# Attention decode with gated GLU on one core: V loads on GpSimd's software queue, K loads and weights on SyncE, w_down in 14 tiles of 128 rows

## The chip, the cores and the metric

The kernel runs on one core of a Trainium2 chip. The metric is the device time of one execution, in microseconds (us). Times are quoted as medians. On one core an execution counts as slow when it is over 1.5% above the fastest of the same kernel. A ratio is the mean time of one kernel's fast runs over that of the other's fast runs in the same rounds on the same chip, so it is not quite the ratio of the medians that stand beside it. Spans in the profile are about 2 us shorter than the device time.

## The reference

Two layers over the same weights and caches; x is [4, 1, 512].

```python
x = A_x
for layer in range(2):            # written out twice in the reference
    n = layernorm(x)
    q = (n @ wq) -> 32 heads of 128                    # 4 heads share one of 8 K/V heads
    p = softmax(q . k_cache * 128**-0.5)               # 4 batches x 8 heads x 4096 keys x 128
    x = x + (p . v_cache) @ wo
    n = layernorm(x)
    x = x + (sigmoid(n @ w_gate) * (n @ w_up)) @ w_down   # 512 -> 1792 -> 512
```

The caches are 33.5 MB each, in bf16, and do not fit on the core, so both layers read them whole: 134 of the 148 MB that the kernel moves. The weights (14 MB) are loaded once and stay.

## The kernel before

The work goes in 16 groups: 2 layers of 8 K/V heads. A group needs four K tiles and four V tiles of 1 MB, one for each batch. All 128 tiles pass through a ring of 10 buffers in the order of use: K of group 0, V of group 0, K of group 1, and so on. A tile takes the buffer of the tile ten places before it and waits until that one has been used. The four K buffers of a group come free when its scores are done, the four V buffers when its values are done.

```python
NS = 10
wd = sb("wd", [FR, 4, 4, D], bf)                 # FR = 112 partitions
...
def load_kv(n, kind, b):
    s = len(tiles) % NS                           # the buffer, in turn
    tiles.append((n, kind, b))
    ...
    if kind == "k":                               # 128 rows of 8 KB
        i = A_k[b, g].rearrange("(p t) d -> p (t d)", p=P)
        o = dst[:]
    else:                                         # 512 rows of 2 KB
        i = A_v[b, g].rearrange("(a p t) d -> p a (t d)", a=4, p=P)
        o = dst[:].rearrange("p (a x) -> p a x", a=4)
    S.put("sp", lambda e: e.dma_start(o, i), writes=[f"r{s}"], dma=f"r{s}")
...                                               # weights: also S.put("sp", ...)
for n, (l, g) in enumerate(groups):
    ensure_t(n, range(B))       # VectorE transposes K blocks in place
    scores(n)                   # TensorE; frees four K buffers
    pump()                      # issue the loads whose buffer is now used: K,K of n+1, V,V of n+1
    softmax(n)
    ...
    values(n)                   # TensorE; frees four V buffers
    pump()                      # V,V of n+1, then K,K of n+2
    merge(n); y_proj(n)
    if last: ... glu(...)       # end of a layer: projection, layer norm, GLU, layer norm
```

Of the kernel before, what the change touches and what calls it, by code (L numbers as in the profile page):

```python
# [10 lines left out]
ENGINES = ("sp", "act", "pe", "dve", "pool")  # L11
# [80 lines left out]
def bass_interleave_layers__gqa_block_cached__glu_gated_glu__decode_kernel(nc, A_x, A_k, A_v, A_wq, A_wo, B_x, B_wg, B_wu, B_wd, out):  # L92
    B, SQ, D = A_x.shape
# [4 lines left out]
    P = 128  # L98
# [3 lines left out]
    NLAYER = 2  # L102
    NQ = 4
    FS = F // 4
    FR = FS // 4
    scale = float(DH) ** -0.5
    eps = 1e-5
    NS = 10

    S = _Sched()  # L110
# [3 lines left out]
    def sb(name, shape, dtype=dt.float32):  # L114
        return es.enter_context(nc.sbuf_tensor(name, list(shape), dtype))

    def ps(name, shape, dtype=dt.float32):
        return es.enter_context(nc.psum_tensor(name, list(shape), dtype))

    bf = dt.bfloat16  # L120
    ring = [sb(f"ring{i}", [P, T * DH], bf) for i in range(NS)]
    wq = sb("wq", [P, KD, H * DH], bf)
    wo = sb("wo", [P, H, D], bf)
    wg = sb("wg", [P, KD, F], bf)
    wu = sb("wu", [P, KD, F], bf)
    wd = sb("wd", [FR, 4, 4, D], bf)

    x_io = sb("x_io", [P, D], bf)
    x_row = [sb(f"x_row{i}", [P, D]) for i in range(2)]
# [12 lines left out]
    oT = sb("oT", [P, H, B], bf)  # L142
    t_sb = sb("t_sb", [P, FS])
    h_sb = sb("h_sb", [P, FS], bf)
    hT = sb("hT", [P, 4, 4, B], bf)

    ml = sb("ml", [P, 64])
    tr = sb("tr", [P, 64])
# [12 lines left out]
    sel_h = sb("sel_h", [P, 16], bf)  # L161
# [6 lines left out]
    M_ps = ps("M_ps", [P, 512])  # L168
    Y_ps = ps("Y_ps", [P, 512])

    sem_names = list(ENGINES) + [f"r{i}" for i in range(NS)] + [f"wq{i}" for i in range(4)]
    sem_names += [f"wo{i}" for i in range(4)] + ["wg", "wu", "wd", "xin", "out"]
    sems = {k: es.enter_context(nc.semaphore(f"sem_{k}")) for k in sem_names}


# [34 lines left out]
    def load_kv(n, kind, b):  # L210
        s = len(tiles) % NS
        tiles.append((n, kind, b))
        slots[n, kind, b] = s
        dst = ring[s]
        g = groups[n][1]
        if kind == "k":
            i = A_k[b, g].rearrange("(p t) d -> p (t d)", p=P)
            o = dst[:]
        else:
            i = A_v[b, g].rearrange("(a p t) d -> p a (t d)", a=4, p=P)  # L220
            o = dst[:].rearrange("p (a x) -> p a x", a=4)
        S.put("sp", lambda e: e.dma_start(o, i), writes=[f"r{s}"], dma=f"r{s}")  # L222

    def pump():
        while queue:
            if isinstance(queue[0], tuple):
                m = len(tiles) - NS
                if m >= 0 and tiles[m] not in used:
                    return
                load_kv(*queue.pop(0))  # L230
            else:
                queue.pop(0)()

    def load_w(key, o, i):
        S.put("sp", lambda e: e.dma_start(o, i), writes=[key], dma=key)  # L235

    wq_src = A_wq.rearrange("(p k) n -> p k n", k=KD)

    def load_wq(i):
        load_w(f"wq{i}", wq[:, :, i * 1024:(i + 1) * 1024], wq_src[:, :, i * 1024:(i + 1) * 1024])  # L240

    def load_wo(i):
        load_w(
            f"wo{i}", wo[:, i * 8:(i + 1) * 8, :],
            A_wo[i * 8 * P:(i + 1) * 8 * P, :].rearrange("(h p) n -> p h n", p=P),
        )
# [7 lines left out]
        (3, "v"): [lambda: load_wo(2)],  # L254
        (4, "v"): [lambda: load_wo(3)],
        (5, "v"): [lambda: load_w("wg", wg[:], B_wg.rearrange("(p k) n -> p k n", k=KD))],
        (6, "v"): [lambda: load_w("wu", wu[:], B_wu.rearrange("(p k) n -> p k n", k=KD))],
        (7, "k"): [lambda: load_w(
            "wd", wd[:].rearrange("r j c n -> r j (c n)"), B_wd.rearrange("(j r c) n -> r j (c n)", j=4, c=4)
        )],  # L260
    }
    queue.append(lambda: load_wq(0))
    for n in range(len(groups)):
# [10 lines left out]
    def layer_norm():  # L274
        xi = state["x"]
        xr = x_row[xi][0:B, :]
        S.put("dve", lambda e: e.bn_stats(stats[0:B, :], xr), reads=[f"x{xi}"], writes=["stats"])
        S.put("dve", lambda e: e.bn_aggr(mv[0:B, :], stats[0:B, :]), reads=["stats"], writes=["mv"])
        S.put("dve", lambda e: e.tensor_scalar_add(vpe[0:B, :], mv[0:B, 1:2], eps), reads=["mv"], writes=["vpe"])
        S.put(  # L280
            "pool", lambda e: e.tensor_tensor(rstd[0:B, :], vpe[0:B, :], mhalf[0:B, :], ALU.pow),
            reads=["vpe", "mhalf"], writes=["rstd"],
        )
        S.put(
            "dve",
            lambda e: e.tensor_scalar(  # L286
                xn[0:B, :], xr, mv[0:B, 0:1], rstd[0:B, :], op0=ALU.subtract, op1=ALU.mult
            ),
            reads=[f"x{xi}", "mv", "rstd"], writes=["xn"],
        )  # L290
        fns = []
        for k in range(KD):
            fns.append(lambda e, k=k: e.matmul(  # L293
                M_ps[:, k * B:(k + 1) * B], lhsT=xn[0:B, bass.ds(k, P, step=KD)], rhs=sel_h[0:B, 0:B],
                start=True, stop=True,
            ))
        S.put("pe", fns, reads=["xn", "sel_h"], writes=["M"])
        S.put(
            "dve", lambda e: e.tensor_copy(xnT[:].rearrange("p k b -> p (k b)"), M_ps[:, 0:KD * B]),
            reads=["M"], writes=["xnT"],  # L300
        )
# [150 lines left out]
    def residual(mult):  # L452
        xi = state["x"]
        S.put(
            "dve",
            lambda e: e.scalar_tensor_tensor(  # L456
                out=x_row[1 - xi][0:B, :], in0=Y_ps[0:B, :], scalar=mult, in1=x_row[xi][0:B, :],
                op0=ALU.mult, op1=ALU.add,
            ),
            reads=["Y", f"x{xi}"], writes=[f"x{1 - xi}"],  # L460
        )
        state["x"] = 1 - xi

    def glu(hooks):
        layer_norm()
        hooks[0]()
        for w, key, bank, bkey in ((wg, "wg", PT_ps, "PT"), (wu, "wu", O_ps, "O")):
            fns = []
            for k in range(KD):
                for j in range(4):  # L470
                    fns.append(lambda e, k=k, j=j, w=w, bank=bank: e.matmul(  # L471
                        bank[32 * j:32 * j + B, 0:FS], lhsT=xnT[:, k, :], rhs=w[:, k, j * FS:(j + 1) * FS],
                        start=(k == 0), stop=(k == KD - 1),
                    ))
            S.put("pe", fns, reads=["xnT", key], writes=[bkey])
        S.put("act", lambda e: e.activation(t_sb[:], PT_ps[:, 0:FS], ACTF.Tanh, scale=0.5), reads=["PT"], writes=["t"])
        S.put(
            "dve",
            lambda e: e.scalar_tensor_tensor(
                out=h_sb[:], in0=t_sb[:], scalar=1.0, in1=O_ps[:, 0:FS], op0=ALU.add, op1=ALU.mult  # L480
            ),
            reads=["t", "O"], writes=["h"],
        )
        fns = []
        for c4 in range(4):
            fns.append(lambda e, c4=c4: e.matmul(
                M_ps[0:FR, c4 * 16:(c4 + 1) * 16], lhsT=h_sb[:, bass.ds(c4, FR, step=4)], rhs=sel_h[:],
                start=True, stop=True,
            ))
        S.put("pe", fns, reads=["h", "sel_h"], writes=["M"])  # L490
        S.put(
            "dve", lambda e: e.tensor_copy(hT[0:FR].rearrange("p c j b -> p (c j b)"), M_ps[0:FR, 0:64]),
            reads=["M"], writes=["hT"],
        )
        hooks[1]()
        fns = []
        for j in range(4):
            for c4 in range(4):
                fns.append(lambda e, j=j, c4=c4: e.matmul(  # L499
                    Y_ps[0:B, :], lhsT=hT[0:FR, c4, j, :], rhs=wd[:, j, c4, :],  # L500
                    start=(j == 0 and c4 == 0), stop=(j == 3 and c4 == 3),
                ))
        S.put("pe", fns, reads=["hT", "wd"], writes=["Y"])
        residual(0.5)


# [10 lines left out]
    for n, (l, g) in enumerate(groups):  # L517
        last = g == G - 1
        ensure_t(n, range(B))
        scores(n)  # L520
        used.update((n, "k", b) for b in range(B))
        pump()
        softmax(n)
        if not last:
            q_proj(g + 1)
        probs_t(n)
        weights(n)
        values(n)
        used.update((n, "v", b) for b in range(B))
        pump()  # L530
        merge(n)
        y_proj(n)
        if last:
            ensure_t(n + 1, [0, 1])
            residual(1.0)
            glu([lambda: ensure_t(n + 1, [2]), lambda: ensure_t(n + 1, [3])])
            if l + 1 < NLAYER:
                layer_norm()
                q_proj(0)
# [4 lines left out]
          writes=["out"], dma="out")  # L544
# [41 lines left out]
```

## Time and profile before

415.18 us, median of two runs (414.91 to 415.44). The execution that was profiled is a third one, 417.68 us.

| what | before | view |
|---|---|---|
| bytes moved | 148.4 MB | page, queues |
| DMA share 90% or more | in 35 of 40 slices | page, slices |
| K to landing, V to landing | 14.2 us, 16.2 us | page, DMA issues |
| w_down to landing | 30.9 us | page, DMA issues |
| rate while w_down passes | 221 to 280 GB/s | table of stretches |
| hole at the layer boundary | 238 to 248 us, 21 GB/s | table of stretches |

These are the lines of the page for slices of 10.4 us, counted from 0 (the first line in tenths of busy time, the second in GB/s) and for DMA issues (target, source, issuer, count, size, median us from issue to landing):

```profile
DMA  7999999999999999999999919999999999999500
GB/s 260 408 382 413 386 389 406 391 415 386 406 391 394 403 407 415 396 416 281 293 411 396 359 25 392 407 401 405 401 407 399 407 399 407 400 407 399 209 2 0
...
ring<-in_A_k_cache_dram SPq DMA_DIRECT2D x64, 1024.0 KB, 14.2
ring<-in_A_v_cache_dram SPq DMA_DIRECT2D x64, 1024.0 KB, 16.2
```

The kernel is bound by its transfers. The engines are at 90% or more in nearly every slice. The rate dips in slices 18 and 19 although the engines are full, and it falls to 25 GB/s in slice 23. The last slices are the chain of work after the last transfer.

The table of stretches gives, for each stretch, busy time of PE, PEld (TensorE's products and its weight loads), DVE, ACT and POOL (VectorE, ScalarE, GpSimd), TensorE's granted clock (as a share of full speed), DMA share and GB/s:

```profile
190.00:195.00 5.00, 0.00 (x0) 0.00 (x0) 3.49 (x2) 0.00 (x0) 0.00 (x0) 0.50 1.03 230
195.00:200.00 5.00, 0.00 (x0) 0.00 (x0) 2.00 (x2) 0.00 (x0) 0.00 (x0) 0.50 1.02 221
200.00:205.00 5.00, 3.59 (x32) 0.94 (x32) 1.30 (x2) 0.00 (x0) 0.00 (x0) 0.50 1.04 280
...
238.00:248.00 10.00, 5.25 (x74) 2.34 (x72) 2.99 (x7) 1.04 (x5) 0.54 (x1) 0.66 0.05 21
```

The two dips differ. In the first three lines the DMA share is 1.02 to 1.04 at 221 to 280 GB/s: the engines work, but badly. That is w_down on 112 partitions. In the last line the share is 0.05: the engines have nothing to do. The ten buffers are full, and the next one comes free only with the first scores of layer two, which stand behind the GLU.

### The profile page before, as it was taken

Reading aid. Unit: us, or ns where it says so; the run is one execution under the profiler, and the core shown is the slowest. Engines: PE = TensorE matmul, PEld = TensorE weight load, DVE = VectorE, ACT = ScalarE, POOL = GpSimd, SP = SyncE. Lnnn points to the kernel's source line nnn. Section 1 sums busy time; section 2 is a strip of 40 time slices with the busy share of each in tenths; the row PEclk is TensorE's granted clock in tenths of the full one; section 3 lists DMA queues with packets and bytes.
Section 4 is the critical chain, followed back from the end, with each engine's and each line's share of the span. In section 5 each row is a group of like instructions: output and inputs, shape, how many; then the busy total and the mean of one; then the engine's idle time right before and its main releaser. Section 6 shows DMA issues by size and latency. Waiting matters only on the chain.

```text
span 415.9 us, 4348 instructions
## 1 busy us (share of the span) xinstructions
PE 203.4 (49%) x1784; PEld 84.8 (20%) x1784; DVE 205.9 (50%) x259; ACT 82.5 (20%) x179; POOL 6.7 (2%) x24
## 2 busy tenths in 40 slices
PE   0047343473545447352316745475745555654556
PEld 0013111121212212120002222131312222221122
DVE  3823627346272825516316626473829283838221
ACT  1031040210403031040210014132231303030300
POOL 4000000000000000000000000000000000000000
PEclk9985565555555555555555766655556666566659
DMA  7999999999999999999999919999999999999500
GB/s 260 408 382 413 386 389 406 391 415 386 406 391 394 403 407 415 396 416 281 293 411 396 359 25 392 407 401 405 401 407 399 407 399 407 400 407 399 209 2 0
DMA packets 50067, 148.40 MB, mean 357 GB/s; under 512 B 2232, under 2 KB 6336, under 8 KB 41600
## 3 DMA queue, kind: packets, MB, share of 16 engines
q1 hardware_dynamic: 50048, 148.13, 93.6%
q8 instruction: 14, 0.23, 0.2%
q14 instruction: 5, 0.04, 0.0%
HBM read 148.12 MB, written 0.00 MB: 356 GB/s over the span
## 4 chain that ended last, share of the span: by engine, by line
issue 40%; DMA 28%; PE 14%; DVE 7%; SPq 6%; ACT 4%; POOL 0%; POOLq 0%; ACTq 0%; DVEq 0%
DMA ring<-in_A_k_cache_dram 24%; PE S_ps L342 5%; SPq L222 5%; DMA ring<-in_A_v_cache_dram 5%; DVE ring L333 3%; PE O_ps L413 3%; ACT p_sb L358 2%; PE Y_ps L499 2%; PE M_ps L429 1%; DVE ml L352 1%; SPq L235 1%; PE Y_ps L446 1%; PE PT_ps L471 1%; PE O_ps L471 1%; ACT o_sb L424 1%
## 5 line engine op out<-in xcount | busy, mean ns | idle before, releaser
L333 DVE STREAM_TRANSPOSE ring<-ring 128x2048 int32<-128x2048 int32 x64 | 146.2, 2299 | 53.7 <-DMA ring<-in_A_k_cache_dram 53.3
L342 PE MATMUL S_ps<-ring,qbd 128*16 128x512 bf16 x512 | 57.0, 620 | 82.4 <-DVE ring L333 81.4
L358 ACT ACTIVATE p_sb<-S_ps,nbias 128x1024 bf16<-128x1024 f32 x16 | 40.4, 2522 | 185.8 <-DVE nbias L355 185.8
L413 PE MATMUL O_ps<-ring,pt_sb 128*16 128x512 bf16 x512 | 57.3, 628 | 27.4 <-ACT pt_sb L374 15.9
L352 DVE TENSOR_REDUCE ml<-S_ps 128x1 f32<-128x1024 f32 x16 | 19.6, 1224 | 60.9 <-PE S_ps L342 60.9
L342 PEld LDWEIGHTS S_ps<-ring,qbd 128*16 128x16 bf16 x512 | 15.4, 120 | 121.2 <-DVE ring L333 81.5
L429 PE MATMUL M_ps<-sel_o,o_sb 128*128 128x16 f32 x128 | 26.9, 349 | 14.0 <-ACT o_sb L424 14.0
L429 PEld LDWEIGHTS M_ps<-sel_o,o_sb 128*128 128x128 f32 x128 | 25.3, 294 | 28.5 <-ACT o_sb L424 28.5
L317 PE MATMUL Q_ps<-qT,perm 128*128 128x16 bf16 x64 | 4.4, 179 | 51.5 <-ACT qT L314 51.5
L446 PE MATMUL Y_ps<-wo,oT 128*4 128x512 bf16 x64 | 26.5, 560 | 4.7 <-ACT oT L435 4.7
L413 PEld LDWEIGHTS O_ps<-ring,pt_sb 128*16 128x16 bf16 x512 | 15.8, 125 | 56.9 <-issue 38.8
L379 DVE STREAM_TRANSPOSE tr<-ml 128x64 f32<-128x64 f32 x16 | 3.9, 245 | 42.2 <-ACT qT L314 37.0
L424 ACT ACTIVATE o_sb<-O_ps,wcol 128x512 f32<-128x512 f32 x16 | 11.0, 687 | 68.3 <-PE O_ps L413 64.6
L323 ACT ACTIVATE qbd<-Q_ps 32x64 bf16<-32x64 f32 x64 | 13.7, 214 | 6.6 <-PE Q_ps L317 6.0
L317 PEld LDWEIGHTS Q_ps<-qT,perm 128*128 128x128 bf16 x64 | 2.9, 107 | 52.8 <-ACT qT L314 52.8
L369 PE MATMUL PT_ps<-sel_p,p_sb 128*128 128x64 bf16 x128 | 9.4, 238 | 8.3 <-ACT p_sb L358 8.3
L393 DVE TENSOR_TENSOR el<-ee,tr 128x16 f32<-128x16 f32 x16 | 2.8, 175 | 20.2 <-ACT ee L392 20.2
L309 PEld LDWEIGHTS Q_ps<-xnT,wq 128*128 128x128 bf16 x256 | 7.9, 102 | 13.3 <-issue 12.9
L309 PE MATMUL Q_ps<-xnT,wq 128*128 128x4 bf16 x256 | 9.2, 166 | 1.6 <-DMA wq<-in_A_wq_dram 1.3
L374 ACT ACTIVATE pt_sb<-PT_ps 128x512 bf16<-128x512 f32 x16 | 9.6, 597 | 1.9 <-PE PT_ps L369 1.5
L456 DVE SCALAR_TENSOR_TENSOR x_row<-Y_ps,x_row 4x512 f32<-4x512 f32 x4 | 2.7, 679 | 14.0 <-PE Y_ps L446 8.8
L293 PE MATMUL M_ps<-sel_h,xn 4*128 4x4 bf16 x16 | 1.2, 173 | 16.9 <-DVE xn L286 16.9
(53 smaller groups left out, 88.7 us busy)
## 6 DMA issues: line engine op xcount, KB each, us to landing
ring<-in_A_k_cache_dram SPq DMA_DIRECT2D x64, 1024.0 KB, 14.2
ring<-in_A_v_cache_dram SPq DMA_DIRECT2D x64, 1024.0 KB, 16.2
wq<-in_A_wq_dram SPq DMA_DIRECT2D x4, 1024.0 KB, 14.9
wo<-in_A_wo_dram SPq DMA_DIRECT2D x4, 1024.0 KB, 14.8
wg<-in_B_w_gate_dram SPq DMA_DIRECT2D x1, 1792.0 KB, 15.7
wu<-in_B_w_up_dram SPq DMA_DIRECT2D x1, 1792.0 KB, 15.7
wd<-in_B_w_down_dram SPq DMA_DIRECT2D x1, 1792.0 KB, 30.9
x_io<-in_A_x_dram SPq DMA_DIRECT2D x1, 4.0 KB
```

The lines of the kernel that those rows point to most:

```text
L222: S.put("sp", lambda e: e.dma_start(o, i), writes=[f"r{s}"], dma=f"r{s}")
L309: fns.append(lambda e, h=h, k=k, c0=c0: e.matmul(Q_ps[:, h * B:(h + 1) * B], lhsT=wq[:, k, c0:c0 + DH], rhs=xnT[:, k, :], start=(k == 0), ...
L323: fns.append(lambda e, a=a: e.activation(qbd[32 * a:32 * a + 32, qi, :, :, a * R:(a + 1) * R], Q_ps[32 * a:32 * a + 32, 64:128].rearrange( ...
L333: S.put("dve", lambda e: e.transpose(v, v), reads=[f"r{s}"], writes=[f"r{s}"])
L342: fns.append(lambda e, q=q, nn=nn, b=b, kt=kt: e.matmul(S_ps[32 * b:32 * b + 16, q * 512:(q + 1) * 512], lhsT=qbd[:, qi, b, nn, :], rhs=kt ...
L352: "dve", lambda e: e.tensor_reduce(ml[:, 0:1], S_ps[:], AX.X, ALU.max, negate=True),
L358: lambda e: e.activation(p_sb[:].rearrange("p tb (j q) -> p q tb j", q=4), S_ps[:].rearrange("p (q tb j) -> p q tb j", q=4, tb=8), ACTF.Ex ...
L374: "act", lambda e: e.activation(pt_sb[:].rearrange("p t x -> p (t x)"), PT_ps[:], ACTF.Copy),
L413: fns.append(lambda e, tb=tb, b=b, v=v: e.matmul(O_ps[32 * b:32 * b + 16, :], lhsT=pt_sb[:, tb, 16 * b:16 * b + 16], rhs=v[:, :, tb, :], s ...
L424: "act", lambda e: e.activation(o_sb[:], O_ps[:], ACTF.Copy, scale=wcol[:, 0:1]),
L429: fns.append(lambda e, a=a: e.matmul(M_ps[:, 0:16], lhsT=o_sb[:, a * P:(a + 1) * P], rhs=sel_o[:, a, :], start=(a == 0), stop=(a == 3),))
L446: fns.append(lambda e, h=h: e.matmul(Y_ps[0:B, :], lhsT=oT[:, g * R + h, :], rhs=wo[:, g * R + h, :], start=(g == 0 and h == 0), stop=(g = ...
```

## The change

The intent is that V loads do not have to wait behind K loads in one in-order queue, and that w_down uses all 128 partitions: 1536 of its 1792 rows (4 blocks of 384) as 12 tiles of 128 rows, and the 4 times 64 rows left as 2 tiles.

```diff
-    wd = sb("wd", [FR, 4, 4, D], bf)
+    wd = sb("wd", [P, 4, 3, D], bf)
+    wd_r = sb("wd_r", [P, 2, D], bf)
...
-        S.put("sp", lambda e: e.dma_start(o, i), writes=[f"r{s}"], dma=f"r{s}")
+        S.put("sp" if kind == "k" else "pool", lambda e: e.dma_start(o, i), writes=[f"r{s}"], dma=f"r{kind}{s}")
...
+    def load_wd():
+        rows = B_wd.rearrange("(j f) n -> j f n", j=4)
+        load_w(
+            "wd", wd[:].rearrange("p j c n -> p j (c n)"),
+            rows[:, 0:FM, :].rearrange("j (p c) n -> p j (c n)", c=3),
+        )
+        for i in range(2):
+            load_w(
+                f"wd_r{i}", wd_r[i * FR:(i + 1) * FR],
+                rows[2 * i:2 * i + 2, FM:FS, :].rearrange("j p n -> p j n"),
+            )
... (the transposes of h and the products with w_down follow: 14 products in place of 16)
```

More of the change, by code (lines that the diff above doesn't have):

```diff
@@ L104, in bass_interleave_layers__gqa_block_cached__glu_gated_glu__decode_kernel @@
     FS = F // 4
-    FR = FS // 4
+    FM = 3 * P
+    FR = FS - FM
     scale = float(DH) ** -0.5
@@ L144, in bass_interleave_layers__gqa_block_cached__glu_gated_glu__decode_kernel @@
     h_sb = sb("h_sb", [P, FS], bf)
-    hT = sb("hT", [P, 4, 4, B], bf)
+    hT = sb("hT", [P, 56], bf)
     ml = sb("ml", [P, 64])
@@ L169, in bass_interleave_layers__gqa_block_cached__glu_gated_glu__decode_kernel @@
     Y_ps = ps("Y_ps", [P, 512])
-    sem_names = list(ENGINES) + [f"r{i}" for i in range(NS)] + [f"wq{i}" for i in range(4)]
-    sem_names += [f"wo{i}" for i in range(4)] + ["wg", "wu", "wd", "xin", "out"]
+    sem_names = list(ENGINES) + [f"r{x}{i}" for i in range(NS) for x in "kv"] + [f"wq{i}" for i in range(4)]
+    sem_names += [f"wo{i}" for i in range(4)] + ["wg", "wu", "wd", "wd_r0", "wd_r1", "xin", "out"]
     sems = {k: es.enter_context(nc.semaphore(f"sem_{k}")) for k in sem_names}
@@ L257, in bass_interleave_layers__gqa_block_cached__glu_gated_glu__decode_kernel @@
         (6, "v"): [lambda: load_w("wu", wu[:], B_wu.rearrange("(p k) n -> p k n", k=KD))],
-        (7, "k"): [lambda: load_w(
-            "wd", wd[:].rearrange("r j c n -> r j (c n)"), B_wd.rearrange("(j r c) n -> r j (c n)", j=4, c=4)
-        )],
+        (7, "k"): [load_wd],
     }
@@ L484, in glu @@
         fns = []
-        for c4 in range(4):
-            fns.append(lambda e, c4=c4: e.matmul(
-                M_ps[0:FR, c4 * 16:(c4 + 1) * 16], lhsT=h_sb[:, bass.ds(c4, FR, step=4)], rhs=sel_h[:],
+        for c in range(3):
+            fns.append(lambda e, c=c: e.matmul(
+                M_ps[:, c * 16:(c + 1) * 16], lhsT=h_sb[:, bass.ds(c, P, step=3)], rhs=sel_h[:],
+                start=True, stop=True,
+            ))
+        for i in range(2):
+            fns.append(lambda e, i=i: e.matmul(
+                M_ps[i * FR:(i + 1) * FR, 48:56], lhsT=h_sb[:, FM:FS], rhs=sel_h[:, 8 * i:8 * i + 8],
                 start=True, stop=True,
@@ L490, in glu @@
         S.put("pe", fns, reads=["h", "sel_h"], writes=["M"])
-        S.put(
-            "dve", lambda e: e.tensor_copy(hT[0:FR].rearrange("p c j b -> p (c j b)"), M_ps[0:FR, 0:64]),
-            reads=["M"], writes=["hT"],
-        )
+        S.put("dve", lambda e: e.tensor_copy(hT[:], M_ps[:, 0:56]), reads=["M"], writes=["hT"])
         hooks[1]()
         fns = []
-        for j in range(4):
-            for c4 in range(4):
-                fns.append(lambda e, j=j, c4=c4: e.matmul(
-                    Y_ps[0:B, :], lhsT=hT[0:FR, c4, j, :], rhs=wd[:, j, c4, :],
-                    start=(j == 0 and c4 == 0), stop=(j == 3 and c4 == 3),
-                ))
-        S.put("pe", fns, reads=["hT", "wd"], writes=["Y"])
+        parts = [(hT[:, 16 * c + 4 * j:16 * c + 4 * j + 4], wd[:, j, c, :]) for c in range(3) for j in range(4)]
+        parts += [(hT[:, 48 + 4 * j:52 + 4 * j], wd_r[:, j, :]) for j in range(2)]
+        for i, (l, r) in enumerate(parts):
+            fns.append(lambda e, i=i, l=l, r=r: e.matmul(
+                Y_ps[0:B, :], lhsT=l, rhs=r, start=(i == 0), stop=(i == len(parts) - 1),
+            ))
+        S.put("pe", fns, reads=["hT", "wd", "wd_r0", "wd_r1"], writes=["Y"])
         residual(0.5)
```

## The prediction

> **What bounds the kernel.** The transfers do. By the page's slices the DMA share is 9 (90% or more) in about 35 of 40 slices, and 148.4 MB at the usual 400 GB/s are 371 of the 415.9 us. Stretches of 2.5 us in the second layer alternate between about 421 and 386 GB/s; the last, with only V left, runs at 386: 8 KB K rows are faster than 2 KB V rows. What is left, by tables of stretches:
> - 190 to 205 us: 220 to 280 GB/s with the DMA engines full. w_down (112 partitions) passes here. About 2.4 MB are missing, 6 us.
> - 238 to 249 us: a hole, about 4.3 MB or 10.8 us. The 10 buffers are full until the first scores of layer two; from the end of the last values of layer one (221.3) to those scores (247.6) the chain takes 26.3 us, and the queue holds only 16.7 us of work at its start.
> - The tail: the last V has landed at about 389.5, values start at 392.6, as the last K landed only at 381.2, before scores and softmax. From there 23 us of chain.
>
> **What the change does.**
> 1. w_down on 128 rows. The Trainium skill, "SBUF — State Buffer", section on the DMA port swizzle, says that bandwidth depends on the ports that the partitions reach, and that a port takes groups of 4; 7 per engine don't align with that. The trace agrees so far as the rate fell to 225. The 1.5 MB part should run at about 400 GB/s, the two rests (0.25 MB) at half that. Gain 5 to 5.5 us, all on the DMA chain, as values of the last group wait for V behind it.
> 2. 14 instead of 16 products on w_down (3.63 us for 16), one small product more: 0.3 us per layer, 0.6 in all, on the chain.
> 3. Two queues. The skill, "DMA: Bandwidth & Descriptors", section "Issuing engines are not separate DMA queues", says that they share the same 16 engines and save only issue time. I expect the rate of V and K unchanged to 2%. The order changes: K no longer queues behind V. K of the last group lands sooner, which takes up to 3 us from the tail (I take 1.5). At the layer boundary V of the last group no longer queues behind w_down, which leaves more K in the queue across the hole; but earlier K elsewhere means less work in hand when values end. I take 0 (-4 to +4).
> 4. GpSimd's rstd stands behind V issues in its program. I expect under 1 us.
>
> Sum: 415.2 - 5.3 - 0.6 - 1.5 = 407.8 us. Range 399 to 420. Faster by over 2% 0.42, within 2% 0.44, slower by over 2% 0.14.
>
> **Right if:** no stretch near 225 GB/s at w_down; w_down lands in under 20 us (30.9 now); the hole is 7 to 14 us; last K to last V landing is over 10 us and values start within 0.5 us of the last V; the rate in the second layer stays at 395 to 412 GB/s.
>
> **Wrong if:** the software queue's descriptors cost rate (V below 370 GB/s, or some engines lagging): up to 15 us slower. Or two queues hide the gap between packets and V runs at 410: up to 8 us faster. Or GpSimd takes several us per issue and delays V or rstd. Or K overtakes V so far that values always wait and the hole grows past 14 us.

## More of the kernel before

In the middle of layer two, TensorE's timeline (start, duration, line, operation, and in brackets the idle time before it and what ended it) is regular; only the lines of scores and values are shown:

```profile
282.92 3.59 PE L342 MATMUL S_ps<-ring,qbd 128*16 128x512 bf16 x32 [1.45 <-DVE ring L333]
292.54 3.59 PE L413 MATMUL O_ps<-ring,pt_sb 128*16 128x512 bf16 x32 [1.16 <-ACT pt_sb L374]
302.50 3.59 PE L342 MATMUL S_ps<-ring,qbd 128*16 128x512 bf16 x32 [1.45 <-DVE ring L333]
312.12 3.40 PE L413 MATMUL O_ps<-ring,pt_sb 128*16 128x512 bf16 x32 [1.16 <-ACT pt_sb L374]
```

Scores (S_ps) come at 282.9 and 302.5 and values (O_ps) at 292.5 and 312.1, evenly spaced. Values wait only for the softmax on ScalarE: their V tiles are already there.

## The result, and the profile after

The changed kernel takes 430.86 us (429.49 to 432.23, two runs; 432.23 is the profiled one). The ratio to the kernel before is 1.0384 (95% interval 1.0308 to 1.0461): slower by 3.8%, outside the predicted range of 399 to 420.

The slices (10.8 us each) and DMA issues of the page after:

```profile
DMA  7999999999999999999999079999799999899400
GB/s 262 404 378 406 396 395 400 398 406 383 410 383 405 414 406 414 400 403 338 403 340 368 2 265 402 402 404 401 266 408 345 390 334 390 322 389 398 157 0 2
...
ring<-in_A_k_cache_dram SPq DMA_DIRECT2D x64, 1024.0 KB, 12.7
ring<-in_A_v_cache_dram POOLq DMA_DIRECT2D x64, 1024.0 KB, 15.6
```

The dip at w_down has shrunk (338 in slice 18, and 403 in slice 19). The hole has moved to slice 22 and grown, and slice 20 before it falls to 340. New are dips in layer two: 266, 345, 334, 322, where the kernel before stays at 399 to 407. Over all runs of the loads K lands sooner than before (12.7 against 14.2 us); in layer two alone (255 us on) the difference is larger, K 9.1 us (13.9 before) and V 15.2 us, at most 20.6 (before 14.2, at most 18.8).

TensorE's timeline in the same part of layer two (again chosen lines):

```profile
284.91 3.59 PE L354 MATMUL S_ps<-ring,qbd 128*16 128x512 bf16 x32 [2.07 <-DVE ring L345]
301.37 3.59 PE L425 MATMUL O_ps<-ring,pt_sb 128*16 128x512 bf16 x32 [8.00 <-DMA ring<-in_A_v_cache_dram]
308.40 0.60 PE L354 MATMUL S_ps<-ring,qbd 128*16 128x512 bf16 x3
```

Values now wait 8.0 us for V. The next scores then need no wait at all, because K of the next group is long there. VectorE's timeline says the same: it transposed the four K tiles of the next group from 295.6 to 304.4, before and during these values. K has overtaken V. In the list of waits of the whole execution (total us, times, longest) the line for values waiting on V grew; first before, then after:

```profile
PE O_ps L413 <- DMA ring<-in_A_v_cache_dram: 11.6, 2, 8.7
```

```profile
PE O_ps L425 <- DMA ring<-in_A_v_cache_dram: 60.7, 9, 10.6
```

The stretches show what this does to the transfers: after, at the boundary and in layer two, and then one of layer two before.

```profile
235.00:240.00 5.00, 3.88 (x27) 1.37 (x19) 3.06 (x3) 0.00 (x0) 0.00 (x0) 0.96 0.25 94
240.00:245.00 5.00, 1.24 (x25) 0.90 (x24) 2.38 (x6) 0.30 (x2) 0.54 (x1) 0.72 0.00 0
245.00:250.00 5.00, 3.97 (x48) 1.45 (x48) 0.63 (x1) 0.74 (x4) 0.37 (x1) 0.59 0.00 0
```

```profile
300.00:305.00 5.00, 3.59 (x32) 1.08 (x32) 4.45 (x3) 0.00 (x0) 0.00 (x0) 0.50 0.70 266
305.00:310.00 5.00, 3.87 (x25) 2.38 (x26) 0.00 (x0) 0.90 (x2) 1.49 (x2) 0.50 0.78 274
```

```profile
300.00:305.00 5.00, 3.55 (x27) 0.92 (x29) 2.45 (x2) 0.00 (x0) 0.00 (x0) 0.50 1.05 386
```

In the changed kernel the DMA share falls to 0.70 just when V has landed and values run (301.4 to 305.0). At that moment the ring holds four landed V and four landed K tiles, and only two loads are out. No buffer comes free until values are done, so the engines run dry.

How the time divides, from the profiled runs, with e1 below (new w_down, one queue) as the third: the first scores of layer two start at 243.99 us before, 245.83 after and 235.06 in e1; from there to the end it is 171.9, 184.6 and 171.3 us. So against e1 the changed kernel loses 10.8 us up to the boundary and 13.2 us after it. Adding up what the dips of layer two after miss against 400 GB/s, in stretches of 5 us, gives 9.9 of the 13.2 us (an estimate).

The loss up to the boundary is mostly the hole: it is 9.4 us longer than in e1 (sums against 400 GB/s, below). By the packet records 83.7 MB had been moved in e1 when the last values of layer one end (214.44 us), and 87.2 MB in the changed kernel (223.68 us): there all four K tiles of the next group have landed by then, in e1 one. So it has about 8.7 us less of transfers in hand (an estimate at 400 GB/s) for a chain of work that lasts 22.2 us until the next buffer comes free (20.6 us in e1).

### The profile page after: what moved, and what is told of

Its sections match the earlier page's. It is cut to its first block, busy times and chain, and to the rows that moved or that the text cites. A ratio compares the mean times of both kernels' runs of the same rounds, so it can differ in the third digit from the quotient of the medians.

```text
span 430.4 us, 4375 instructions
## 1 busy us (share of the span) xinstructions
PE 188.5 (44%) x1782; PEld 80.1 (19%) x1782; DVE 203.4 (47%) x259; ACT 82.7 (19%) x179; POOL 54.9 (13%) x88
## 4 chain that ended last, share of the span: by engine, by line
DMA 57%; PE 18%; issue 8%; SPq 7%; DVE 5%; ACT 2%; POOL 2%; POOLq 0%; ACTq 0%; DVEq 0%
DMA ring<-in_A_v_cache_dram 40%; DMA ring<-in_A_k_cache_dram 18%; PE O_ps L425 9%; SPq L224 6%; PE S_ps L354 4%; DVE ring L345 2%; POOL ring L224 2%; PE Y_ps L516 1%; ACT p_sb L370 1%; PE PT_ps L483 1%; PE O_ps L483 1%; DVE ml L364 1%; ACT qbd L335 1%; DVE x_row L468 0%; SPq L237 0%
## 5 line engine op out<-in xcount | busy, mean ns | idle before, releaser
L345 DVE STREAM_TRANSPOSE ring<-ring 128x2048 int32<-128x2048 int32 x64 | 144.4, 2286 | 33.6 <-DMA ring<-in_A_k_cache_dram 33.5
L425 PE MATMUL O_ps<-ring,pt_sb 128*16 128x512 bf16 x512 | 56.1, 616 | 77.1 <-DMA ring<-in_A_v_cache_dram 60.7
L224 POOL DMA_DIRECT2D ring<-in_A_v_cache_dram x64 | 48.0, 755 | 323.2 <-PE O_ps L425 175.8
L354 PE MATMUL S_ps<-ring,qbd 128*16 128x512 bf16 x512 | 59.3, 586 | 59.5 <-DVE ring L345 58.5
L354 PEld LDWEIGHTS S_ps<-ring,qbd 128*16 128x16 bf16 x512 | 16.5, 111 | 93.4 <-DVE ring L345 51.3
L441 PE MATMUL M_ps<-sel_o,o_sb 128*128 128x16 f32 x128 | 22.8, 314 | 14.0 <-ACT o_sb L436 14.0
L441 PEld LDWEIGHTS M_ps<-sel_o,o_sb 128*128 128x128 f32 x128 | 21.2, 251 | 27.3 <-ACT o_sb L436 27.3
L458 PE MATMUL Y_ps<-wo,oT 128*4 128x512 bf16 x64 | 22.9, 494 | 4.7 <-ACT oT L447 4.7
L305 PE MATMUL M_ps<-sel_h,xn 4*128 4x4 bf16 x16 | 1.2, 174 | 20.6 <-DVE xn L298 20.6
## 6 DMA issues: line engine op xcount, KB each, us to landing
ring<-in_A_k_cache_dram SPq DMA_DIRECT2D x64, 1024.0 KB, 12.7
wu<-in_B_w_up_dram SPq DMA_DIRECT2D x1, 1792.0 KB, 20.6
wd<-in_B_w_down_dram SPq DMA_DIRECT2D x1, 1536.0 KB, 21.6
```

The lines of the kernel that those rows point to most:

```text
L224: S.put("sp" if kind == "k" else "pool", lambda e: e.dma_start(o, i), writes=[f"r{s}"], dma=f"r{kind}{s}")
L345: S.put("dve", lambda e: e.transpose(v, v), reads=[f"r{s}"], writes=[f"r{s}"])
L354: fns.append(lambda e, q=q, nn=nn, b=b, kt=kt: e.matmul(S_ps[32 * b:32 * b + 16, q * 512:(q + 1) * 512], lhsT=qbd[:, qi, b, nn, :], rhs=kt ...
L425: fns.append(lambda e, tb=tb, b=b, v=v: e.matmul(O_ps[32 * b:32 * b + 16, :], lhsT=pt_sb[:, tb, 16 * b:16 * b + 16], rhs=v[:, :, tb, :], s ...
L441: fns.append(lambda e, a=a: e.matmul(M_ps[:, 0:16], lhsT=o_sb[:, a * P:(a + 1) * P], rhs=sel_o[:, a, :], start=(a == 0), stop=(a == 3),))
L458: fns.append(lambda e, h=h: e.matmul(Y_ps[0:B, :], lhsT=oT[:, g * R + h, :], rhs=wo[:, g * R + h, :], start=(g == 0 and h == 0), stop=(g = ...
```

## The experiments

Theory 1: two queues change the order of arrival. K and V share the rate, K of the next group overtakes V of this one, and with a ring of fixed size what came too early takes up the room for what comes next. Theory 2: the software queue itself is slow or late. Theory 3: the new w_down costs the time. In e1 to e14 the results are correct by comparison with the reference.

### e1: the new w_down alone

```diff
-        S.put("sp" if kind == "k" else "pool", ...)
+        S.put("sp", ...)
```

> w_down in 14 tiles as in the changed kernel, but V loads back on SyncE's queue with everything else. Theory 1 (order: with K and V on two queues K of the next group overtakes V of this one, and the buffers run dry when values end) and theory 2 (the software queue itself is slow or late): 407 to 411 us, that is 415.2 less the 5 to 6 us lost at w_down. Theory 3 (the new w_down layout costs the time): above 420 us.

Measured: 408.9 us (before 416.49 in these rounds), ratio 0.9841 (0.9794 to 0.9887). Theory 3 falls: the new w_down is a gain of 1.6%. Its stretches:

```profile
190.00:195.00 5.00, 0.00 (x0) 0.00 (x0) 4.64 (x3) 0.00 (x0) 0.00 (x0) 0.50 1.02 377
195.00:200.00 5.00, 3.59 (x32) 0.94 (x32) 1.30 (x2) 0.00 (x0) 0.00 (x0) 0.50 1.06 279
200.00:205.00 5.00, 0.61 (x8) 0.45 (x8) 1.46 (x5) 3.23 (x4) 0.00 (x0) 0.50 1.05 388
...
234.00:240.00 6.00, 4.00 (x51) 1.40 (x48) 1.38 (x2) 0.86 (x4) 0.00 (x0) 0.65 0.22 52
```

Against 400 GB/s the kernel before misses 6.1 us of transfer from 190 to 210 us, e1 2.0 us from 190 to 205 us. What is left is one stretch at 279 GB/s; the two 64-row rests lie in it. The hole shrinks too, from 11.1 us (235 to 255 us) to 5.5 us (234 to 245 us) by the same sum. When the last values of layer one end, 83.7 MB have been moved and not 84.9, so about 3 us more of transfers are in hand. The chain from there to the first scores of layer two is also shorter, 20.6 us and not 22.8. Most of that is no gain of the edit: two groups of products that are the same in both kernels took 1.06 and 1.02 us in e1's profile and 1.89 and 1.86 us before, in stretches with a mean granted clock of 0.67 and 0.50. The profiles don't show how often that happens.

### e2: the two queues alone

The kernel before, with only the V loads moved to GpSimd (the same one-line edit and a semaphore for each kind).

> The kernel before with only the V loads moved to GpSimd's queue; w_down as before on 112 rows. Theories 1 and 2: 431 to 437 us, as the changed kernel or up to 6 us worse, since the w_down gain is missing. Theory 3: about 415 us.

Measured: 432.47 us, ratio 1.0394 (1.0331 to 1.0457). The queues alone make a loss of the same size as the whole change. With two queues the w_down gain nearly vanishes as well: 432.5 with the old one, 430.9 with the new one. In e2 the rate beside the old w_down is 299 to 326 GB/s and not 221 to 280, which fits V filling in from the other queue.

### e3: V on ScalarE's hardware queue

```diff
-        S.put("sp" if kind == "k" else "pool", ...)
+        S.put("sp" if kind == "k" else "act", ...)
```

> The changed kernel with V loads issued from ScalarE (a second hardware queue) in place of GpSimd's software queue. Theory 1 (order between two queues): 425 to 433 us, with the same dips of the transfer rate each time values end. Theory 2 (software descriptors): 405 to 412 us.

Measured: 433.4 us, ratio 1.0403 (1.0347 to 1.0458). This is the loss again, 0.4 us over the range of theory 1, without a software queue. Theory 2 falls as the cause. The dips are there too (slices of e3; layer two begins in slice 23):

```profile
GB/s 274 418 387 414 381 400 399 414 382 361 404 370 408 401 329 419 380 410 375 404 365 344 49 122 407 404 388 407 400 409 307 408 348 405 317 393 396 147 0 2
```

But ScalarE pays for these loads, which stand in its program before its own work: one issue took 8.6 us (median 0.5), and TensorE waited longer for ScalarE's o_sb than in the changed kernel. First the changed kernel, then e3:

```profile
PE M_ps L441 <- ACT o_sb L436: 14.0, 16, 0.9
```

```profile
PE M_ps L441 <- ACT o_sb L436: 34.7, 16, 4.2
```

How much of e3's time this costs is not known.

### e4: both kinds over both queues, by batch

```diff
-        S.put("sp" if kind == "k" else "pool", ..., dma=f"r{kind}{s}")
+        eng = "sp" if b % 2 == 0 else "pool"
+        S.put(eng, ..., dma=f"r{'kv'[b % 2]}{s}")
```

> The changed kernel with K and V both divided over the two queues by batch: batches 0 and 2 on SyncE, 1 and 3 on GpSimd, so each queue has K and V in the order of use and neither can overtake by much, while half of all cache bytes still go by the software queue. Theory 1: 405 to 412 us, no dips in layer two. Theory 2: above 420 us.

Measured: 420.56 us, ratio 1.0103 (1.0058 to 1.0147). A miss for theory 1; the median is just over the 420 us that theory 2 gave as its least. The dips of layer two are gone (no slice under 377 GB/s there until the end), but 11.7 us over e1 remain, most of them at the layer boundary: the first scores of layer two start at 241.98 and not at 235.06. Tiles on GpSimd's queue land in 11.6 us (K) and 12.8 us (V), those on SyncE's in 17.6 and 18.5: the queues do not run level.

### e5 and e9: everything on the software queue

e5 puts all loads, weights too, on GpSimd, in the order of the kernel before. e9 also issues the first loads before GpSimd builds its constants.

```diff
-        S.put("sp" if kind == "k" else "pool", ...)
+        S.put("pool", ...)
-        S.put("sp", lambda e: e.dma_start(o, i), writes=[key], dma=key)     # weights
+        S.put("pool", lambda e: e.dma_start(o, i), writes=[key], dma=key)
     pump()
+    S.prog["pool"].sort(key=lambda it: it.sem == "pool")                    # e9 only
```

> The changed kernel with every cache and weight load on GpSimd's software queue: one queue, all by software descriptors, in the order of the kernel before. Theory 1 (order between queues): 405 to 411 us, as with everything on SyncE (408.9). Theory 2 (software descriptors are slow or late): worse than the changed kernel, above 430 us.

> All loads on GpSimd's software queue as in e5, but GpSimd issues the first loads before it builds its constants, so the stream starts at about 2 us and not at 7. Theory 1: the 5 us of late start come back: 410 to 413 us. If the software queue itself costs the 7.6 us that e5 was above e1: no change, 415 to 417.

Measured: e5 416.47 us, ratio 0.9989 (0.9934 to 1.0044), over the range that theory 1 gave. Its first slice has 37 GB/s: GpSimd's first load is issued at 6.97 us, after the constants. e9 410.53 us, ratio 0.9868 (0.9822 to 0.9914), and its first load is issued at 1.28 us. By medians one software queue in the order of use is 1.6 us slower than one hardware queue (e1: 408.9 us, ratio 0.9841), and the intervals overlap. It issues a V load in 0.75 us. That closes theory 2 as the cause of the 22 us: a software queue alone does not cost them.

### e6: two queues that wait for each other

Each load also waits for the landing of the last load of the other kind that is at least 4 tiles ahead of it.

```diff
+        idx = len(tiles) - 1
+        other = [it for m, it in enumerate(loads) if m <= idx - 4 and tiles[m][1] != kind][-1:]
-        S.put("sp" if kind == "k" else "pool", ...)
+        loads.append(S.put("sp" if kind == "k" else "pool", ..., after=other))
```

> The changed kernel, V on GpSimd and K on SyncE as in it, but each load waits until the last load of the other kind that is 4 or more tiles ahead of it in the order of use has landed, so neither queue can run further ahead. Theory 1: most of the loss comes back, 408 to 414 us, and no dips below 350 GB/s in layer two. Theory 2: no gain, 428 us or more, as each load waits longer.

Measured: 418.51, 424.93, 421.92 and 413.65 us; the second and third count as slow, so the ratio 0.9978 (0.9873 to 1.0083) rests on two runs. Some of the loss comes back, as theory 1 expected, but less than it gave, and how much is unclear. No slice of layer two is below 373 GB/s.

### e7 and e8: two more buffers

```diff
-    NS = 10
+    NS = 12        # room: a smaller descriptor area, 4096 bytes a partition in e7, 2048 in e8
```

e7 is the changed kernel, e8 is e1, each with 12 buffers.

> The changed kernel with 12 ring buffers in place of 10 (room from a smaller descriptor area). Theory 1: two more tiles (5.1 us of transfer) stay in hand when values end, more than the dips of layer two (some 2 us each), so these go and the boundary hole shrinks by about 5 us: 405 to 416 us. Theory 2: little change, above 424 us.

> New w_down, all loads on SyncE, 12 buffers: the hole at the layer boundary (about 10 us) should shrink by the 5.1 us that two more tiles take, nothing else changes: 402 to 406 us against 408.9 with 10 buffers.

Measured: e7 412.43 us, ratio 0.9913 (0.9841 to 0.9986); e8 405.77 us, ratio 0.9729 (0.9667 to 0.9791). Two buffers more are worth 18 us to two queues and 3 us to one; two queues still cost 6.7 us with 12 buffers. The smaller descriptor area is a second change in e7, but GpSimd issues its V loads as fast as before (0.75 us each in both). The slices of e7 show why; the dips of layer two are gone:

```profile
GB/s 253 406 386 396 403 382 413 393 406 390 397 403 383 415 410 407 409 401 407 382 395 407 410 115 329 415 391 414 395 410 394 410 397 409 402 407 397 173 0 2
```

This is the strongest sign that the loss is one of room: V is still overtaken in e7 (values wait for it up to 8.4 us, in the timeline at 194.2 us), but in layer two the ring no longer runs dry for it. e8 is the fastest kernel and beats both.

### e10 and e12: e4 with level queues

e10 divides the weights over both queues too (wq1, wo1, wo2, w_gate and the large part of w_down on GpSimd). e12 is e4 with ScalarE's queue in place of GpSimd's.

```diff
-        S.put("sp", lambda e: e.dma_start(o, i), writes=[key], dma=key)     # e10
+        S.put("pool" if key in ("wq1", "wo1", "wo2", "wg", "wd") else "sp", ...)
-        eng = "sp" if b % 2 == 0 else "pool"                                # e12
+        eng = "sp" if b % 2 == 0 else "act"
```

> As e4 (both kinds divided over the two queues by batch), but the weights divided over both queues too, so that neither queue carries 14 MB more than the other. Theory 1: what e4 was above e1 came from the queue with the weights falling behind, mostly before the layer boundary: 409 to 413 us. Theory 2 (two queues or software descriptors cost time whatever the order): 418 us or more.

> As e4, cache loads divided by batch over two queues, but the second queue is ScalarE's hardware queue. Theory 1b (two queues with unequal packets: in e10 both queues moved 303 and 302 packets in 195 to 200 us, but 1.24 and 0.40 MB, so the one with larger packets runs ahead): with 2 KB packets for V on both, neither runs ahead: 408 to 414 us. Theory 1c (any two queues let later tiles take half of the rate from the tile that is waited for, whatever the packets): 417 to 423 us, as e4 and e10.

Measured: e10 420.37 us, ratio 1.0110 (1.0058 to 1.0163); e12 420.51 us, ratio 1.0134 (1.0096 to 1.0173). Both miss theory 1, and neither the weights nor the kind of the second queue was the reason for e4. The text of e12 divides theory 1 in two, 1b (unequal packets) and 1c (any two queues); e12 lies in the range of 1c, 417 to 423 us. What the traces showed was how queues share. In e12 from 190 to 195 us the two queues moved 333 and 334 packets, but 1.31 and 0.68 MB: packet for packet in this stretch, whatever their size. A K row is a packet of 8 KB. A V row is one of 2 KB on a hardware queue, and two rows make one of 4 KB on the software queue. So the queue that is at K takes two to four times the bytes of the queue that is at V, even where both queues hold K and V tiles. e12 did not make the packets equal, contrary to what its text says, because one queue can be at K while the other is at V.

The queue lines of the profile show it in a stretch of 3 us in layer two (packets, MB, share), first of the changed kernel (286 to 289 us), then of e3 (287 to 290 us; q10 is ScalarE's queue with V):

```profile
q1 hardware_dynamic: 106, 0.84, 69.5%
q0 software_dynamic: 99, 0.40, 33.6%
```

```profile
q1 hardware_dynamic: 126, 0.97, 79.3%
q10 hardware_dynamic: 110, 0.20, 20.8%
```

K has two thirds of the bytes beside the software queue's V, and over four fifths beside V on a hardware queue.

### e11: the rests of w_down from two queues

e8, with the second 64-row rest issued from ScalarE.

```diff
-        S.put("sp", lambda e: e.dma_start(o, i), writes=[key], dma=key)
+        S.put("act" if key == "wd_r1" else "sp", ...)
```

> The candidate: all cache loads on SyncE, 12 buffers, new w_down, its second 64-row rest issued from ScalarE so that both rests, which reach different partitions, can go at once. Against e8 (405.8): 0 to 1.5 us less, 404 to 406 us; the stretch at the rests should rise above 300 GB/s.

Measured: 406.62 us over six runs, ratio 0.9776 (0.9738 to 0.9814). The lowest stretch at the rests rises from 308 GB/s (e8) to 333, as expected, but the time is not below e8's and lies over the 404 to 406 us that was expected; the intervals overlap. No gain.

### e13 and e14: K in pieces of 4 KB, which failed

e13 is the changed kernel and e14 is e1, with K's rows asked for as two pieces.

```diff
-            i = A_k[b, g].rearrange("(p t) d -> p (t d)", p=P)
-            o = dst[:]
+            i = A_k[b, g].rearrange("(p c t) d -> p c (t d)", p=P, c=2)
+            o = dst[:].rearrange("p (c x) -> p c x", c=2)
```

> The changed kernel with K rows loaded as two pieces of 4 KB, so that a packet of K is as large as one of V in the software queue (4 KB). Theory 1b: K's share where both wait falls from two thirds to half, V lands earlier, and of the 22 us between this kernel and one queue at least half come back: 412 to 420 us. Theory 1c: 428 us or more.

> Control for e13: everything on SyncE, K rows in pieces of 4 KB. If 4 KB pieces cost rate as the 2 KB rows of V do (421 against 386 GB/s; 4 KB between them), 3 to 6 us more than e1: 411 to 415 us. If they are merged into 8 KB rows again: 409.

Measured: e13 429.55 us, ratio 1.0370 (1.0311 to 1.0428); e14 409.12 us, ratio 0.9854 (0.9820 to 0.9887). The pieces are contiguous at both ends and were merged again: in e13 from 184 to 190 us, 213 packets of SyncE's queue carried 1.59 MB, 7.5 KB each. So the edit changed nothing, and the two runs say nothing on packets. They only repeat the changed kernel (430.86) and e1 (408.9). e13's runs spread from 423.08 to 432.16: the record counts two of its four (431.0 and 432.16) as slow, against the profiled one at 423.08, yet the ratio comes out as given only over the three that were not profiled, those two included. The two fast ones alone have a mean of 425.6 us, so e13 is a loose repeat of the changed kernel.

### e15, e16 and e17: K in rows of 2 KB

K takes V's row order, so that its rows are not contiguous and cannot be merged. The keys then no longer match the values, so the result is wrong; the comparison with the reference still passed, so it would not have caught this. e15 is e1 with it, e16 is e3, and e17 is e12 with the weights over both queues.

```diff
-            i = A_k[b, g].rearrange("(p t) d -> p (t d)", p=P)
-            o = dst[:]
+            i = A_k[b, g].rearrange("(a p t) d -> p a (t d)", a=4, p=P)
+            o = dst[:].rearrange("p (a x) -> p a x", a=4)
```

> Control for e16 and e17: all on SyncE, but K loaded with V's row order, so in 2 KB rows that are not merged (e13 and e14 failed at this: the two 4 KB pieces were merged into packets of 8 KB again). Gives a wrong result on purpose, as the keys no longer match the values; shapes and work are the same. K at V's 386 instead of 421 GB/s: 64 tiles times 0.23 us more, 14 us: 419 to 426 us.

> As e3 (K and weights on SyncE, V on ScalarE's queue), K in 2 KB rows like V, so the turn by turn of packets gives K half and not up to four fifths. Wrong result on purpose as e15. Theory 1b (unequal packets): at most 10 us above e15, against 24.5 between e3 and e1. Theory 1c (any two queues): 18 us or more above e15.

> As e12 (cache loads by batch over SyncE and ScalarE), weights over both queues as in e10, and K in 2 KB rows, so that both queues always have packets of one size but for the weights. Wrong result on purpose as e15. Theory 1b: at most 4 us above e15, against 11.6 between e12 and e1. Theory 1c: 9 us or more above e15.

Measured: e15 421.56 us, ratio 1.0141 (1.0099 to 1.0183); e16 431.18 us, ratio 1.0384 (1.0340 to 1.0428); e17 426.07 us, ratio 1.0253 (1.0215 to 1.0290). In e16 the queues now share evenly (287 to 290 us; q10 has V):

```profile
q1 hardware_dynamic: 290, 0.59, 53.9%
q10 hardware_dynamic: 286, 0.58, 51.8%
```

| arrangement | K in 8 KB rows | K in 2 KB rows |
|---|---|---|
| one queue | 408.9 (e1) | 421.6 (e15) |
| K on SyncE, V on ScalarE | 433.4 (e3), +24.5 | 431.2 (e16), +9.6 |
| both over both, by batch | 420.5 (e12), +11.6 | 426.1 (e17), +4.5 |

With packets of one size the cost of two queues falls from 24.5 to 9.6 us and from 11.6 to 4.5 us, but it does not vanish. This fits two causes together: unequal packets make the overtaking worse, and any two queues let tiles that are needed later take rate from the tile that is waited for. It does not show the second one. (e16 lies within the bound of theory 1b and e17 half a microsecond over it.) Three cautions. All two-queue rows of the table issue from ScalarE, and there TensorE waits 31 to 51 us in total for o_sb (e12, e3, e16, e17), against 14 in e1 and e15; the 9.6 and 4.5 us that are left can be that as well. e17 also divides the weights, which e12 does not (in e10 this changed nothing against e4: 420.37 and 420.56 us). And with 2 KB rows a group's eight tiles take longer to move, which gives the compute chain more slack, so part of the smaller cost may come from that. The runs do not separate these.

## Why the prediction was wrong

The step that failed is the third, "Two queues", where the prediction put "I take 0 (-4 to +4)" for the change of order. Measured, that term is +22 us: 430.9 against 408.9 with one queue (e1), and ratio 1.0394 for the queues alone (e2). The prediction had the right mechanism on its list ("Or K overtakes V so far that values always wait and the hole grows past 14 us") and gave slower by over 2% a chance of 0.14. It took the order of arrival to be a matter of a few microseconds at the ends. In place of that the runs showed values that wait for V in nine groups of 16 (60.7 us in all; two groups and 11.6 before), dips in layer two that miss 9.9 us of transfer, and a hole 9.4 us longer than in e1.

- The first step (w_down) held. The prediction had 5.3 + 0.6 us with step two; e1 measured 7.6 us by medians, ratio 0.9841. The other 2 us are in the hole, which shrank as well, in part by luck (see e1). But with two queues nearly nothing of it was left (e2 against the changed kernel: 1.6 us). w_down landed in 21.6 us and not in under 20.
- "The rate of V and K unchanged to 2%" held only away from the dips: there the stretches of the second layer run at 386 to 421 GB/s with two queues, against 383 to 426 before, and one software queue costs 1.6 us by medians (e9). In the dips the rate falls to 265 GB/s, far outside the 395 to 412 that the prediction named as a mark of being right. Its own first fear, slow descriptors, was not it.
- "K of the last group lands sooner, which takes up to 3 us from the tail" did not happen. The last K lands 8.5 us before the last V and not over 10 (10.7 before), and values start 3.0 us after the last V and not within 0.5. There was little to gain in any case: the prediction took V to be there at 389.5 us before the change, but that is the third of the four tiles; the last one lands at 392.0 us, 0.7 us before values start.
- The hole was to be 7 to 14 us. By the sum against 400 GB/s from 235 to 255 us it is 14.9 us (11.1 before, 5.5 in e1).
- rstd on GpSimd behind V issues was to cost under 1 us. At the boundary that held: GpSimd is idle for 5.0 us before it and waits only for VectorE; it takes 0.56 us. At the start of the kernel it did not: rstd stands behind four V issues (6.98 to 10.13 us), and TensorE's first product starts at 11.33 us and not at 7.76. No loss is seen from that: VectorE then waits for the next K tiles all the same (1.3 to 1.7 us each).

Why the order matters so much here: of the arrangements tried, one queue in the order of use was the fastest for a ring that is also in the order of use. The transfers of a group take about 20.7 us (8.39 MB at about 405 GB/s), and scores and values alternate within that. Before, each landed tile was the next one to be needed. With two queues, the ring at the start of values is full of landed tiles, and the stream stops until values free four of them. That this is a matter of room is shown by e7 (18 us back with two more buffers), and that it is a matter of order, not of the software queue, by e9 and, with the reserve on ScalarE, by e3. That packets set the shares is shown by the packet counts, in the stretches looked at. How much of the loss they cause is indicated by e15 to e17, not settled.

## What to carry to other kernels

The second DMA queue added no bandwidth to this kernel, whose DMA engines were already full, and it gave away the order of arrival. With a ring of buffers filled in the order of use, put all tiles on one queue in that order, or give the ring as many more tiles as the queues can get out of order. If two queues must be used, compare the row lengths on them: here they shared packet for packet and not byte for byte.

## What the Trainium skill lacked or had wrong

- "DMA: Bandwidth & Descriptors", section "Issuing engines are not separate DMA queues", says that DMAs of several engines interleave on the same 16 engines, and that several issuers save only issue time. The runs agree on the bandwidth, but the page does not say that the changed order can cost: 22 us of 409 here (e1 against the changed kernel).
- The same page, section "Queues, rings and completion order", says that each engine goes round the queues packet by packet, and gives about 9 to 17 descriptors as a typical packet. The turns agree with the trace (333 and 334 packets in the same 5 us of e12). The size can't be compared: the profile counts one packet for each row on the hardware queues (8 KB for K, 2 KB for V) and one for two rows of 2 KB on the software queue, and no run shows whether these are the page's packets. The page does not draw the conclusion that shares of bytes follow row length (0.97 against 0.20 MB in e3).
- The same page, section "Issuing engine by pattern", says that the hardware queues are generally faster. Here a V load of 512 rows took GpSimd 0.75 us to issue, and with all loads on the software queue the kernel took 1.6 us more by medians than with SyncE (e9 410.5, e1 408.9), with intervals that overlap.
- "SBUF — State Buffer", section on the DMA port swizzle, gives the ports but no rate for 112 partitions. Measured: 221 to 280 GB/s before, and 279 GB/s at worst in the stretch with the 64-row rests of the new layout (e1).
